# Last units of the hidden layer put in another order, the reload of db cut into eight, and the transform's middle multiplied through a negated plane

## The chip, the cores and the metric

The kernel runs on one core of one Trainium2 chip. The metric is the time of one execution on the device in microseconds (us); the runs of the kernel before took 1208.77, 1212.85 and 1214.51 us, median 1212.85.

The engines go by the profile's names: PE multiplies matrices (PEld is its weight load), DVE works on vectors, ACT copies and evaluates functions, POOL does vector work and issues the stores, and SP issues the loads. Each engine takes its instructions strictly in order. A transposing load issued by SP appears in SP's row with a long duration, and what SP issues next stands behind it.

## What is computed

The forward value and all gradients of a gated sum of a spectral filter and a two-layer perceptron, 2048 rows by 1024 columns, hidden width 3584, bfloat16 in and out:

```python
g = sigmoid((x * gate_w).sum(-1, keepdims=True))
a = irfft2(rfft2(x.astype(float32)) * (w_r + 1j * w_i))
h = relu(x @ w1 + b1); h = h * h
b = h @ w2 + b2            # here x is B_x, with no gradient
out = g * a + (1 - g) * b
_, vjp = jax.vjp(f, A_x, w_r, w_i, w1, b1, w2, b2, gate_w); vjp(grad_out)
```

## The kernel before, in words

**The stages.** The rows of x and of the incoming gradient come in, are turned for the matmuls, and the row transforms of the spectral part write z_scr in DRAM; db, the gradient that goes into the perceptron, is stored to db_scr. Then the *hidden layer* runs (`mlp_in`, one generator) and beside it, step by step, the spectral part (`fft_mid`, then `fft_out`). After it the gradients of w1 and w2 and the output of the second layer are made (`mlp_grads`), from h2T_scr and dhT_scr, the hidden values and their gradients, which the hidden layer has stored. The "first pass" is the hidden layer, the "second pass" what comes after it.

**The hidden layer.** The hidden width is 28 chunks of 128, that is 14 pairs `fp` (0 to 13, `LAST` is 13). Rows are 4 blocks `s` of 512, that is 2 halves `sp`. Pairs 0 and 1, and half 0 of the last pair, are made plainly (`forth`, L740). The others go in *units* `(fp, sp)` of seven chains (`p1` to `p7`, L847), a Strassen-like scheme: each unit multiplies sums of quarters of w1 (`w_sums`, L836, four sums on DVE per pair) with sums of quarters of x (`x_sums`), and DVE's `rest` (L863) adds the pieces and the bias into `rT`. With it come, for the unit before, four `pd` chains of eight matmuls (`grads`, L747), which DVE evicts into `dhT` (L751). The order written out is `seq`: (2,0), (2,1), (3,0) ... (12,0), (12,1), (13,1). The sums for an odd pair lie in the last two rows of the tile `dbn`, those of x in the rest: while the units run, dbn (16 row blocks of db) is lent out as `kept`, and after them it is loaded again from db_scr (`again`, L1001): rows 0 to 7 after unit (12,0), rows 8 to 15 after the last unit. Each w1 pair is loaded into w1g (L769) one pair ahead, two buffers.

**What runs beside it.** The middle of the transform, `fft_mid`, makes 32 turns `(m, h)`, 16 pairs of frequencies by two halves. A turn loads z (L393, SP), makes sum and difference `pm` (L413, L414, DVE), multiplies on PE to `px` (L422), copies to x on ACT (L423, and an edge column, L424), multiplies x with the filter w on DVE into tt (L430 with the real part, L431 with imaginary and negated imaginary), joins the products to y (L441, L442; the column at the edge by L438, L439), goes back through PE (L450) to pc (ACT L455, DVE L456, L457), and makes the gradients of the filter (L467 to L471, two products and two sums), which ACT scales into gw. The planes of x are real and imaginary, each of 2 x 256 values and two edge columns.

**What sets the order.** `spread` lets one generator make steps while the other runs, at a given rate of steps per step of the hidden layer, so a step of the transform falls between two chains of a unit. Within an engine the order of the program, as adjusted by explicit ties such as `later["last"]`, is the order of execution. SP takes loads in that order: z, w1g, the transposing loads of w2 (`load_w2`, L183), the reload of db, and the first transposing loads of the second pass (`fetch` from h2T_scr, four into `even` and four into `odd`, also L183). The loads into `even` wait for `later["blocks"]`, the last dhT eviction made within unit (12,0), which the loop of the units sets.

The second pass begins with PE chains on dbn and `even` (L1143, pX and pV), and sums T and S of dbn and `even` on DVE (L1075).

Of the kernel before, what the change touches and what calls it, by code (L numbers as in the profile page):

```python
# [10 lines left out]
P = 128  # L11
BF16 = mybir.dt.bfloat16
FP16 = mybir.dt.float16
FP32 = mybir.dt.float32
ALU = mybir.AluOpType
ACT = mybir.ActivationFunctionType

FDT = FP16
# [123 lines left out]
def kernel(  # L142
# [22 lines left out]
    nc = tc.nc  # L165
# [9 lines left out]
    NT = S // P  # L175
# [8 lines left out]
    ld, st = nc.sync.dma_start, nc.gpsimd.dma_start  # L184
    V, mm = nc.vector.tensor_tensor, nc.tensor.matmul
# [18 lines left out]

    identb = pers.tile([P, P], BF16, name="identb", tag="identb")
    nc.scalar.dma_start(out=identb[:], in_=cten["identb"].ap())
    kf = pers.tile([P, 2, P], FDT, name="kf", tag="kf")
    flip = pers.tile([P, 1], FP32, name="flip", tag="flip")
    cols = lambda n, w, dt=FP32: pers.tile([P] + w, dt, name=n, tag=n)
    gcol, omg, gpg, dgs, dsc = (cols(n, [NT]) for n in ("gcol", "omg", "gpg", "dgs", "dsc"))  # L210
# [114 lines left out]
    def fft_mid(filler):  # L325
# [6 lines left out]

        def edges():

            ed = fb.tile([P, NM, 2, 4], FDT, name="ed", tag="ed")
            low = fb.tile([P, NM, 4], FDT, name="low", tag="low")
            mid = fb.tile([P, 4], FDT, name="mid", tag="mid")
            nc.vector.memset(ed[lanes[1], 0], 0.0)
            col = z_scr[:].rearrange("t c r x h l -> r c h l x t")[:, :, 0, 0]
            for x in range(2):  # L340
                for t in range(2):
                    e = 2 * x + t
                    st(out=ed[lanes[0], :, 0, e], in_=col[:, 0:NM, x, t])
                    st(out=low[lanes[1], :, e], in_=col[:, NM:, 1 - x, t])
                    st(out=mid[lanes[0], e : e + 1], in_=col[:, NM, 1 - x, t : t + 1])
            return ed, low, mid
# [10 lines left out]
        def edges_through(ams, ed, low, mid):  # L357
            tied = lambda ins: after(ins, later["last"], mybir.DependencyClass.NoSync)
            tied(nc.vector.tensor_copy(out=ed[lanes[0], :, 1, :], in_=ed[lanes[0], :, 0, :]))
            tied(nc.vector.tensor_copy(out=ed[lanes[0], 0, 1, :], in_=mid[lanes[0]]))  # L360
            for n in range(2):
                a, b = slice(2 * n, 2 * n + 2), slice(2 - 2 * n, 4 - 2 * n)
                tied(nc.vector.tensor_copy(out=ed[lanes[1], 1:, n, a], in_=low[lanes[1], 1:, a]))
                tied(nc.vector.tensor_scalar(out=ed[lanes[1], 1:, n, b], in0=low[lanes[1], 1:, b], scalar1=-1.0, scalar2=None, op0=ALU.mult))
            sp = fps.tile([P, NM, 2, 4], FP32, name="sp", tag="ps2", bufs=2)
            for h in range(2):
                for m in range(NM // 2):
                    for n in range(2):
                        mm(
                            sp[:, h * NM // 2 + m, n], lhsT=ams[h][:, m, n, :], rhs=ed[:, h * NM // 2 + m, n, :],  # L370
                            start=True, stop=True, skip_group_check=True,
                        )
            ex = fb.tile([P, NM, 2, 2, 2], FDT, name="ex", tag="ex")
            for n in range(2):
                for c in range(2):
                    nc.vector.tensor_copy(
                        out=ex[lanes[n], :, c], in_=sp[lanes[c], :, n, :].rearrange("p m (e t) -> p m t e", e=2)
                    )
            return ex

        def filters(m):
# [33 lines left out]
            return pm  # L415

        def transform(m, h, pm, ex):
            x = fb.tile([P, 2, 2, WL], FDT, name="x", tag="x", bufs=2)
            px = fps.tile([P, 2, 2, HW], FP32, name="px", tag="ps2", bufs=2)
            for c in range(2):  # L420
                for n in range(2):
                    behind(mm(px[lanes[n], c], lhsT=mats[m][:, 0, n, lanes[c]], rhs=pm[:, n], start=True, stop=True), "PE")  # L422
            nc.scalar.copy(out=x[:, :, :, 0:HW], in_=px[:])  # L423
            nc.scalar.copy(out=x[:, :, :, h * HW], in_=ex[:, m, :, :, h])  # L424
            return x

        def products(h, x, w):
            tt = fb.tile([P, 2, 2, 2, WL], FDT, name="tt", tag="tt")
            W = HW + h
            V(out=tt[:, 0, :, :, 0:W], in0=x[:, :, :, 0:W], in1=w[:, 0:1, 0:W].rearrange("p (o t) l -> p o t l", o=1).to_broadcast([P, 2, 2, W]), op=ALU.mult)  # L430
            V(out=tt[:, 1, :, :, 0:W], in0=x[:, :, :, 0:W], in1=w[:, 1:3, 0:W].rearrange("p (o t) l -> p o t l", o=1).to_broadcast([P, 2, 2, W]), op=ALU.mult)  # L431
            return tt

        def joined(h, tt, eh):
            if h:
                nc.scalar.copy(out=eh[:], in_=tt[:, :, :, :, HW])
            else:
                V(out=tt[:, :, 0, :, 0], in0=tt[:, :, 0, :, 0], in1=eh[:, :, 1, :], op=ALU.subtract)  # L438
                V(out=tt[:, :, 1, :, 0], in0=tt[:, :, 1, :, 0], in1=eh[:, :, 0, :], op=ALU.add)  # L439
            y = fb.tile([P, 2, 2, HW], FDT, name="y", tag="y")  # L440
            V(out=y[:, 0], in0=tt[:, 0, 0, :, 0:HW], in1=tt[:, 1, 1, :, 0:HW], op=ALU.subtract)  # L441
            V(out=y[:, 1], in0=tt[:, 0, 1, :, 0:HW], in1=tt[:, 1, 0, :, 0:HW], op=ALU.add)  # L442
            return y

        def back(m, h, y):
# [15 lines left out]

        def grads_of_w(h, x):
            W = HW + h
            XA, XB = (x[:, :, T, 0:W] for T in range(2))
            gs = fb.tile([P, 2, WL], FDT, name="gs", tag="gs", bufs=2)
            t1_ = fb.tile([P, 2, WL], FDT, name="g1", tag="g1")
            V(out=t1_[:, :, 0:W], in0=XB, in1=XA, op=ALU.mult)  # L467
            V(out=gs[:, 0, 0:W], in0=t1_[:, 0, 0:W], in1=t1_[:, 1, 0:W], op=ALU.add)
            t2_ = fb.tile([P, 2, WL], FDT, name="g1", tag="g1")
            V(out=t2_[:, :, 0:W], in0=XB, in1=XA[:, ::-1, :], op=ALU.mult)  # L470
            V(out=gs[:, 1, 0:W], in0=t2_[:, 1, 0:W], in1=t2_[:, 0, 0:W], op=ALU.subtract)  # L471
            return gs

        def grads_out(m, h, gs, gw, done):
# [25 lines left out]
        yield  # L500
        for u, (m, h) in enumerate(turns):
            if h:
                eh = fb.tile([P, 2, 2, 2], FDT, name="eh", tag="eh")
            x = transform(m, h, pm, ex)
            yield
            if u + 1 < len(turns):
                pm = mirrored(turns[u + 1][0], z.pop(u + 1))
            if held:
                done = back(*turns[u - 1], held)
            tt = products(h, x, w)  # L510
            if u + 1 < len(turns):
                m2, h2 = turns[u + 1]
                w = by_groups(h2, wn[m2])
            yield
            held = joined(h, tt, eh)
            yield
            if u:
                grads_out(*turns[u - 1], gs, gw, done)
            gs = grads_of_w(h, x)
            if h:  # L520
                gw = fb.tile([P, 2, LW], BF16, name="gw", tag="gw", bufs=2)
                if m + 1 < NM:
                    wn[m + 1] = filters(m + 1)
            if u + 2 < len(turns):
                z[u + 2] = inputs(*turns[u + 2])
            yield
# [113 lines left out]
    f1, f1_s = pool("f1", "right")  # L640

    cf = f1.tile(list(consts["cf"].shape), FDT, name="cf", tag="cf")
    xs = {}

    def turn_tile(dst, i, src, copy):
# [61 lines left out]
    def mlp_in():  # L707
# [227 lines left out]
                load_w1(2)  # L935
        for _ in w_sums(2, True):
            pass
        seq = [(fp, sp) for fp in range(2, LAST) for sp in range(2)] + [(LAST, 1)]
        more_sums = x_sums(1)
        units_ = [Unit(*u) for u in seq]  # L940
        units_[0].p2()
        for n, u in enumerate(units_):
            fg, pr = divmod(u.fp, NPR)
            if u.sp == 0 and u.fp < LAST:
                load_w1(u.fp + 1)
            u.p1()
            if n:
                units_[n - 1].square(0, u.copy)
            back_(*waiting[0])
            u.p5()  # L950
            yield
            next(more_sums, None)
            u.p6()
            if n:
                units_[n - 1].square(1, u.copy)
            back_(*waiting[1])
            next(more_sums, None)
            ahead_ = w_sums(u.fp + 1, True) if u.sp == 1 and u.fp < LAST else iter(())
            next(ahead_, None)
            yield  # L960
            u.p7()
            back_(*waiting[2])
            next(more_sums, None)
            next(ahead_, None)
            yield
            back_(*waiting[3])
            for _ in ahead_:
# [8 lines left out]
            elif n == 2 * DC + 1:  # L976
                grad_of_b2()
            u.p4()
            u.p3()
            if n + 1 < len(units_):  # L980
                units_[n + 1].p2()
            yield
            waiting = [(u.fp, 2 * u.sp + j, c) for c, j in ((0, 0), (0, 1), (1, 1), (1, 0))]
            if (u.fp, u.sp) == (LAST - 1, 0):
                again(slice(0, 8))
        again(slice(8, NT))
        units_[-1].square(0), units_[-1].square(1)
        more = [(LAST, s, c) for c in range(2) for s in range(2)]
        for this, that in zip(more, waiting):
# [7 lines left out]
        wbs.close()  # L997
        xT_s.close()

    def again(rows_):  # L1000
        ld(out=dbn[:, rows_, :], in_=db_scr[:, rows_, :])  # L1001

    def column_sums(sb_pool, acc, tag):

# [837 lines left out]
```

## Time and profile before

| what | value |
|---|---|
| median of three runs | 1212.85 us (1208.77 to 1214.51) |
| the profiled execution, its own time | 1206.2 us |
| its span, first to last instruction | 1204.4 us |
| mean granted TensorE clock | 0.999 |
| busy PEld, share of the span | 637.2 us, 53% |
| DMA moved | 249.88 MB, mean 207 GB/s |
| loads: z 128 KB, w1g 512 KB, db 2048 KB | 4.1, 5.1, 9.9 us median from issue to landing |

A row of a timeline or queue gives the start in us from the span's beginning, the duration, the engine, the line, the operation, the tile written and those read, and in brackets the idle time just before and what ended it. A row of waits gives who waited for whom, the us in total, how often and the longest. A group of instructions gives after the count the busy time in us, the mean of one in ns and the idle time ahead.

### The profile page before, as it was taken

Reading aid. Unit: us, or ns where it says so; the run is one execution under the profiler, and the core shown is the slowest. Engines: PE = TensorE matmul, PEld = TensorE weight load, DVE = VectorE, ACT = ScalarE, POOL = GpSimd, SP = SyncE. Lnnn points to the kernel's source line nnn. Section 1 sums busy time; section 2 is a strip of 40 time slices with the busy share of each in tenths; the row PEclk is TensorE's granted clock in tenths of the full one; section 3 lists DMA queues with packets and bytes.
Section 4 is the critical chain, followed back from the end, with each engine's and each line's share of the span. In section 5 each row is a group of like instructions: output and inputs, shape, how many; then the busy total and the mean of one; then the engine's idle time right before and its main releaser. Section 6 shows DMA issues by size and latency. Waiting matters only on the chain.

```text
span 1204.4 us, 19697 instructions
## 1 busy us (share of the span) xinstructions
PE 1184.8 (98%) x7379; PEld 637.2 (53%) x7379; DVE 886.4 (74%) x1660; ACT 513.2 (43%) x909; POOL 381.9 (32%) x614
## 2 busy tenths in 40 slices
PE   8999999999999998999999999999999999999997
PEld 5565555444344433444446999998544444444444
DVE  3668887589999878777736666666785777977666
ACT  4668888466666663334423566564110110000000
POOL 0223333766666654564341323321001100000000
PEclk9999999999999999999999999999999999999999
DMA  9977575967585899899995999995899999564531
GB/s 287 302 247 227 168 218 159 202 194 202 175 206 177 248 228 246 177 178 230 197 239 126 238 225 250 238 214 161 255 206 273 270 230 273 161 195 144 184 114 36
DMA packets 328986, 249.88 MB, mean 207 GB/s; under 512 B 188200, under 2 KB 287946, under 8 KB 328122
## 3 DMA queue, kind: packets, MB, share of 16 engines
q1 hardware_dynamic: 283808, 119.99, 46.3%
q0 software_dynamic: 35520, 111.74, 29.4%
q10 hardware_dynamic: 9562, 16.89, 4.3%
q8 instruction: 58, 0.95, 0.3%
q14 instruction: 38, 0.31, 0.1%
HBM read 114.84 MB, written 89.67 MB: 170 GB/s over the span
## 4 chain that ended last, share of the span: by engine, by line
PE 74%; DVE 12%; DMA 5%; issue 3%; ACT 3%; SPq 1%; POOL 1%; DVEq 0%; POOLq 0%
PE pX L1143 15%; PE xX L1439 13%; PE pV L1143 11%; PE pd L747 10%; PE xV L1439 7%; PE ph L847 6%; PE xZ L1439 3%; DMA y_scr<-pc 2%; PE ph L740 1%; PE pui L317 1%; PE pki L576 1%; PE pZ L847 1%; PE pu L317 1%; PE px L422 1%; PE pk L286 1%
## 5 line engine op out<-in xcount | busy, mean ns | idle before, releaser
L747 PE MATMUL pd<-dbT,w2T 128*128 128x512 bf16 x896 | 211.0, 379 | 5.0 <-DVE dhT L751 3.9
L747 PEld LDWEIGHTS <-w2T 128*128 128x128 bf16 x896 | 85.7, 98 | 109.9 <-issue 12.3
L1439 PEld LDWEIGHTS <-dS 128*128 128x128 f16 x686 | 66.5, 98 | 78.6 <-issue 3.0
L751 DVE SCALAR_TENSOR_TENSOR dhT<-pd,rT 128x512 bf16<-128x512 f32 x112 | 76.6, 685 | 41.4 <-PE pd L747 39.3
L1490 POOL DMA_DIRECT2D out_dram<-ot x32 | 17.3, 542 | 257.1 <-DVE ot L1546 128.0
L1556 ACT ACTIVATE w2br<-w2br,dsc 128x512 f32<-128x512 bf16 x8 | 5.8, 723 | 172.8 <-DVE ot L1546 117.4
L1439 PE MATMUL xX<-oT,dS 128*128 128x512 f16 x336 | 76.4, 379 | 0.2 <-DVE eR L1468 0.2
L1159 ACT COPY u<-pX 128x512 f32<-128x512 f32 x56 | 32.8, 585 | 93.2 <-PE pX L1143 87.1
L1439 PEld LDWEIGHTS <-odd 128*128 128x128 bf16 (+1 forms) x462 | 44.8, 98 | 51.5 <-issue 0.9
L1439 PEld LDWEIGHTS <-even 128*128 128x128 bf16 (+1 forms) x448 | 43.7, 98 | 52.6 <-issue 0.7
L1143 PEld LDWEIGHTS <-T 128*128 128x128 f16 x672 | 64.4, 98 | 8.2 <-DVE S L1075 1.2
L864 ACT ACTIVATE rT<-rT 128x512 bf16<-128x512 bf16 x69 | 43.3, 628 | 51.2 <-DVE rT L863 51.0
L732 ACT ACTIVATE h2T<-rT 128x1024 bf16<-128x1024 bf16 x56 | 59.7, 1066 | 0.5 <-DMA h2T_scr<-h2T 0.2
L459 POOL DMA_DIRECT2D y_scr<-pc x64 | 47.0, 736 | 36.7 <-DVE pc L456 28.3
L1163 DVE TENSOR_TENSOR whi<-pV,u 128x512 bf16<-128x512 f32 x28 | 19.3, 690 | 51.0 <-ACT u L1159 50.9
L1143 PEld LDWEIGHTS <-S 128*128 128x128 f16 x336 | 31.8, 98 | 43.2 <-DVE S L1075 3.3
L1143 PEld LDWEIGHTS <-resL 128*128 128x128 bf16 x448 | 43.1, 98 | 4.9
L1143 PEld LDWEIGHTS <-resR 128*128 128x128 f16 (+1 forms) x448 | 42.9, 98 | 5.1 <-issue 0.2
L778 POOL DMA_DIRECT2D h2T_scr<-h2T x28 | 20.6, 736 | 73.6 <-ACT f L274 35.7
L232 POOL DMA_DIRECT2D r<-y_scr x48 | 27.9, 584 | 42.8 <-ACT re L555 27.4
L1143 PEld LDWEIGHTS <-even 128*128 128x128 bf16 (+1 forms) x256 | 24.6, 98 | 31.0 <-issue 2.1
L484 POOL DMA_DIRECT2D out_dram<-gw x64 | 34.3, 541 | 17.3 <-ACT gw L480 10.9
(375 smaller groups left out, 2765.3 us busy)
## 6 DMA issues: line engine op xcount, KB each, us to landing
h2T_scr<-h2T POOLq DMA_DIRECT2D x28, 512.0 KB, 4.4
dhT_scr<-dhT POOLq DMA_DIRECT2D x28, 512.0 KB, 5.6
z<-z_scr SPq DMA_DIRECT2D x64, 128.0 KB, 4.1
y_scr<-pc POOLq DMA_DIRECT2D x64, 128.0 KB, 4.2
ax_scr<-yo POOLq DMA_DIRECT2D x16, 512.0 KB, 5.4
out_dram<-ot POOLq DMA_DIRECT2D x31, 256.0 KB, 3.8
out_dram<-whi POOLq DMA_DIRECT2D x28, 256.0 KB, 5.4
out_dram<-wlo POOLq DMA_DIRECT2D x28, 256.0 KB, 4.6
```

Of the source, the lines that this page charges most:

```text
L232: st(out=a, in_=b) if stored else st(out=b, in_=a)
L317: first_ = mm(pu[:, bank, lo : lo + n], lhsT=ft[:, b, :], rhs=mat[:, o : o + n], start=bool(f_ & 1), stop=bool(f_ & 2), skip_group_check=True,
L459: st(out=columns_of(y_scr, c, h), in_=pc[:, n])
L484: st(out=every(dst_w, k), in_=gw[lanes[n], c_, 0:W1])
L732: after(nc.scalar.activation(h2T, rT, ACT.Square), behind_, mybir.DependencyClass.NoSync)
L747: mm(pd[:], lhsT=w_[:, ec, fc % FGC * P : (fc % FGC + 1) * P], rhs=dbT[:, ec, ss], start=(ec == 0), stop=(ec == DC - 1),)
L751: return STT(out=dhT, in0=pd[:], scalar=2.0, in1=rT, op0=ALU.mult, op1=ALU.mult, accum_out=gb1part[:, fc, sb : sb + 1],)
L847: mm(acc[:], lhsT=lhs[:, t, :], rhs=rhs[:, t, :], start=start and t == 0, stop=t == KH - 1, skip_group_check=True)
L864: nc.scalar.activation(rT, rT, ACT.Relu)
L1143: self.mm = mm(out, lhsT=lhs[:, t, m * P : (m + 1) * P], rhs=rhs[:, t, :], start=start and t + a == 0, stop=t == KH - 1, skip_group_check= ...
L1159: turn["ACT"] = nc.scalar.copy(out=t_[:], in_=self.X[:])
L1439: ins = mm(acc, lhsT=lhs[:, fc, :], rhs=rhs[:, fc, :], start=start and fc == 0, stop=fc == KH - 1 and bias is None, skip_group_check=True,)
```

## The change

Three things are changed; what is computed stays the same. `kf`, a small constant, also moves from a lasting pool to one that ends with the first stage, and the scratch tiles of `edges` now use space of others.

**Units.** The last units run as (10,0), (10,1), (11,0), (12,0), (11,1), (12,1), (13,1). The load of w1g for pair 13 is therefore issued at unit (11,1).

**Reload.** dbn comes back in eight pieces of two row blocks, as the sums in them have been read: four after the chains of unit (12,0)'s successor (11,1), three during the last unit, and one behind it.

**Transform.** x has three planes: negated imaginary, real, imaginary. The negated one is one more ACT multiply of px. The products take planes (real, imaginary) with the real part of the filter, and (negated imaginary, real) with its imaginary part, so that y is one sum of 1024 values. The edge column is joined first (`en`) and added to y once. The gradients of the filter take one product of 1024 values and one sum.

```diff
-        seq = [(fp, sp) for fp in range(2, LAST) for sp in range(2)] + [(LAST, 1)]
+        seq = [(fp, sp) for fp in range(2, LAST - 2) for sp in range(2)]
+        seq += [(fp, sp) for sp in range(2) for fp in (LAST - 2, LAST - 1)] + [(LAST, 1)]
+        freed = seq.index((LAST - 1, 0))
+        def freed_rows(n, low, high):
+            if n == freed + 1:
+                again(slice(2 * low, 2 * low + 2), later["last"])
+            elif n == len(seq) - 1 and high:
+                again(slice(6 + 2 * high, 8 + 2 * high))
...
-            if u.sp == 0 and u.fp < LAST:
+            if (u.fp, u.sp) == (LAST - 2, 1):
+                load_w1(LAST)
+            elif u.sp == 0 and u.fp < LAST - 1:
                 load_w1(u.fp + 1)
...
             u.p5()
+            freed_rows(n, 0, 1)
             yield
             next(more_sums, None)
             u.p6()
+            freed_rows(n, 1, 2)
...
-            ahead_ = w_sums(u.fp + 1, True) if u.sp == 1 and u.fp < LAST else iter(())
-            next(ahead_, None)
+            follows = u.fp + 1 if u.sp == 1 and u.fp < LAST - 2 else {(LAST - 2, 0): LAST - 1, (LAST - 1, 1): LAST}.get((u.fp, u.sp))
+            ahead_ = w_sums(follows, True) if follows else iter(())
+            dealt = ahead_ if (u.fp, u.sp) != (LAST - 2, 0) else iter(())
+            next(dealt, None)
...
+            freed_rows(n, 2, 0)
...
             u.p4()
+            freed_rows(n, 3, 3)
...
-            if (u.fp, u.sp) == (LAST - 1, 0):
-                again(slice(0, 8))
-        again(slice(8, NT))
+        again(slice(NT - 2, NT))
```
```diff
         def transform(m, h, pm, ex):
-            x = fb.tile([P, 2, 2, WL], FDT, name="x", tag="x", bufs=2)
+            x = fb.tile([P, 3, 2, WL], FDT, name="x", tag="x", bufs=2)
...
-            nc.scalar.copy(out=x[:, :, :, 0:HW], in_=px[:])
+            nc.scalar.copy(out=x[:, 1:3, :, 0:HW], in_=px[:])
+            nc.scalar.mul(out=x[:, 0, :, 0:HW], in_=px[:, 1], mul=-1.0)
...
         def joined(h, tt, eh):
+            V(out=y[:], in0=tt[:, 0, :, :, 0:HW], in1=tt[:, 1, :, :, 0:HW], op=ALU.add)
             if h:
-                nc.scalar.copy(out=eh[:], in_=tt[:, :, :, :, HW])
+                V(out=en[:], in0=tt[:, 0, :, :, HW], in1=tt[:, 1, :, :, HW], op=ALU.add)
+                nc.scalar.mul(out=eh[:, 0], in_=en[:, 1], mul=-1.0)
+                nc.scalar.copy(out=eh[:, 1], in_=en[:, 0])
             else:
-                V(out=tt[:, :, 0, :, 0], in0=tt[:, :, 0, :, 0], in1=eh[:, :, 1, :], op=ALU.subtract)
-                V(out=tt[:, :, 1, :, 0], in0=tt[:, :, 1, :, 0], in1=eh[:, :, 0, :], op=ALU.add)
-            V(out=y[:, 0], in0=tt[:, 0, 0, :, 0:HW], in1=tt[:, 1, 1, :, 0:HW], op=ALU.subtract)
-            V(out=y[:, 1], in0=tt[:, 0, 1, :, 0:HW], in1=tt[:, 1, 0, :, 0:HW], op=ALU.add)
+                V(out=y[:, :, :, 0], in0=y[:, :, :, 0], in1=eh[:], op=ALU.add)
...
         def grads_of_w(h, x):
-            V(out=t1_[:, :, 0:W], in0=XB, in1=XA, op=ALU.mult)
-            V(out=gs[:, 0, 0:W], in0=t1_[:, 0, 0:W], in1=t1_[:, 1, 0:W], op=ALU.add)
-            V(out=t2_[:, :, 0:W], in0=XB, in1=XA[:, ::-1, :], op=ALU.mult)
-            V(out=gs[:, 1, 0:W], in0=t2_[:, 1, 0:W], in1=t2_[:, 0, 0:W], op=ALU.subtract)
+            V(out=t_[:, :, :, 0:W], in0=XB, in1=XA, op=ALU.mult)
+            V(out=gs[:, ::-1, 0:W], in0=t_[:, :, 0, 0:W], in1=t_[:, :, 1, 0:W], op=ALU.add)
```

## Prediction

> **What bounds the kernel now.** I read the share of busy time first, then who makes TensorE (PE) wait, then 20 us windows around the change, then the queues there. PE is busy 1184.8 of 1204.4 us at a granted clock of 0.999, and no step of the diff alters a matmul's count or shape. So a gain can only come out of PE's 19.6 us of idle time. From the idle time noted in PE's timeline, 3.4 lie in the first 12 us and 7.0 after 1196 us, untouched by the change. About 9.2 are left, in small pieces but for one place: the window from 440 to 460 us holds 3.92 (20 minus 16.08). The page, the waits of PE and the windows:
>
> ```profile
> PE 1184.8 (98%) x7379; PEld 637.2 (53%) x7379; DVE 886.4 (74%) x1660; ACT 513.2 (43%) x909; POOL 381.9 (32%) x614
> ```
> ```profile
> PE pd L747 <- DVE dhT L751: 3.9, 2, 3.3
> PE pX L1143 <- DVE S L1075: 1.6, 3, 0.7
> PE pd L747 <- DVE rT L863: 1.1, 3, 0.6
> ```
> ```profile
> 420.00:440.00 20.00, 20.00 (x100) 7.91 (x97) 17.16 (x44) 14.79 (x25) 11.62 (x18) 1.00 1.23 170
> 440.00:460.00 20.00, 16.08 (x76) 6.88 (x75) 12.30 (x32) 7.78 (x14) 11.26 (x19) 1.00 1.10 316
> ```
>
> The windows' columns are stretch, length, then busy time of PE, PEld, DVE, ACT and POOL: PE is full until 440, and DVE too drops to 12.30 after it. The reason stands in the queue of the loads (SP), start and duration first:
>
> ```profile
> 404.95 0.33 SPq L1001 DMA_DIRECT2D dbn<-db_scr  x1
> 405.63 8.94 SPq L183 DMA_TRANSPOSE even<-h2T_scr  x1
> 414.68 1.96 SPq L393 DMA_DIRECT2D z<-z_scr  x2
> 416.68 21.53 SPq L183 DMA_TRANSPOSE even<-h2T_scr  x3
> 438.31 2.60 SPq L393 DMA_DIRECT2D z<-z_scr  x4
> ```
>
> Four transposing loads hold SP for 8.94 + 21.53 = 30.4 us. The z loads behind them issue only at 438.31; DVE stands for them, with the hidden layer's evictions (dhT, L751) queued behind, and PE stands for those. DVE's and PE's timelines:
>
> ```profile
> 445.20 0.43 DVE L413 TENSOR_TENSOR pm<-z 128x512 f16<-128x512 f16 x1 [5.36 <-DMA z<-z_scr]
> ...
> 456.39 0.68 DVE L751 SCALAR_TENSOR_TENSOR dhT<-pd,rT 128x512 bf16<-128x512 f32 x1
> ```
> ```profile
> 450.24 3.61 PE L747 MATMUL pd<-dbT,w2T 128*128 128x512 bf16 x16 [0.65 <-DVE dhT L751]
> 457.13 5.34 PE L747 MATMUL pd<-dbT,w2T 128*128 128x512 bf16 x24 [3.27 <-DVE dhT L751]
> ```
>
> **Part 1, order of units and reload in pieces.** The four transposes wait for the dhT of unit (12,0), which comes one unit (about 15 us) earlier. In SP's new order they start near 389 us, back to back; behind them come pieces 1 and 2, two z loads, piece 3, the load of w1g for pair 13, and then pieces and z in turn. The z loads of 438.31 now stand behind no transpose: they issue by about 430 and are needed at 439 to 447. So the 5.36 us wait of DVE goes, and with it the stall: **-3.9 us** on PE. What is late next there: between two dhT stand only two pm and two tt, about 2.2 us of DVE, against 1.7 us of a pd chain with other matmuls between; I leave nothing.
>
> The cost sits in w1g for 13. In before it issues at 390.42, ahead of the transposes. Now it stands behind all four, and its sums (L836) are in DVE's order as before, the first at 415.24. When do four transposes end that start at 389? Pairs of them elsewhere in SP's timeline:
>
> ```profile
> 285.24 6.86 SPq L183 DMA_TRANSPOSE w2T<-in_B_w_dram  x2
> 345.26 7.97 SPq L183 DMA_TRANSPOSE w2T<-in_B_w_dram  x2
> ```
>
> Two such pairs give 14.8 us, ending near 404; the four odd transposes at 453.11 took 20.07, giving 409; the 30.4 us of 405 to 438 gives 419.4. I take 16 to 20 us, as the 280 to 350 pairs stand in the same stage of units. With pieces and z before it, w1g issues at 406 to 411, and lands at its median of 5.1 us, or 7 behind pieces: 411 to 418. PE does not feel it until about 417.9: what stands behind the sums is rT (L863, 416.42), needed for the chain at 419.65, and the dhT at 417.75, needed near 420.5. I take **+0.6 us** (bounds 0 and, from 30.4 us, w1g issued at 421.5 and landed at 428 to 431, +10 to +13).
>
> The eight pieces: issue costs 0.33 to 0.70 us each on SP, which waits anyway. The two 2 MB loads took 9.9 us to land. The first reader of dbn as db is PE's pX at 462.94, and the last piece issues when the last sums are read, about 435.5. Even the 9.9 us of four times the size after that is 445: 17 us of cover, so nothing. If a piece were delayed past 462, it would cost one for one.
>
> The rows of the DMA issues give a load of w1g (512 KB) a median of 5.1 us to landing and one of db (2048 KB) 9.9: four times the data in twice the time, so small pieces do cost more per byte. The Trainium skill, "DMA: Bandwidth & Descriptors", section "Bandwidth", advises batching transfers to 1 MiB or more, which speaks against eight of 512 KB and agrees with those rows. By the fit in that page's section "Anatomy of one DMA" (an estimate) eight would take about 26 us of transfer against 14 for two of 2 MB; if that were on the path the sum would be 12 us worse.
>
> **Part 2, transform with a negated plane.** Per turn (32 turns) DVE loses one y, two g/gs and, on average, no edge operation. The rows of the groups (mean ns after the busy time):
>
> ```profile
> L441 DVE TENSOR_TENSOR y<-tt 128x512 f16<-128x512 f16 x32 | 14.2, 443 | 0.0
> L442 DVE TENSOR_TENSOR y<-tt 128x512 f16<-128x512 f16 x32 | 13.7, 429 | 0.0
> L598 DVE TENSOR_TENSOR tt<-ev,e 128x1024 f16<-128x1024 f16 x16 | 11.1, 691 | 1.5
> ```
>
> 443 + 429 become one like L598, 691 ns: 0.18 saved. Two products g (418 and 431 at h=0) and two sums gs (286 and 340) become one of about 690 and one of about 440: 1475 to 1130, 0.35 saved. At h=0 one of two edge fixes (417, 166) goes; at h=1 one is added. Records overlap by about 0.08, so some 0.25 us a turn, 8 us of DVE in all. DVE is 74% busy and PE does not wait for it but at the places named: **0** on the path. Only the stall near 396 us (0.59, pd waits for rT, the third row of the waits) stands behind a run of such operations, and rT comes 1 to 2 us earlier: **-0.6**.
>
> ACT gains one 128x512 multiply out of PSUM and small copies: L455's 582 ns plus about 0.2, 26 us in all. ACT was 13 to 15 of 20 us busy in the stage, and its own work is not waited for by PE. But the two products now need the negated plane, so x is ready about 0.6 us later; DVE idled at L430 for ACT 4.1 us in 32 turns, and other DVE work stands between. Bounds: 0, and 32 x 0.6 = 19 us if every turn exposed it to PE; the nearest row is the 1.1 us that PE ever waited for rT, so I take 0.
>
> Two places where DVE's new order is worse. (a) At 246.95 pm waits 0.82 for z, issued behind transposes:
>
> ```profile
> 243.90 0.74 DVE L863 SCALAR_TENSOR_TENSOR rT<-pZ,b1col,cu 128x512 bf16<-128x512 f32 x1
> ...
> 246.95 0.81 DVE L413 TENSOR_TENSOR pm<-z 128x512 f16<-128x512 f16 x1 [0.82 <-DMA z<-z_scr]
> ```
>
> In the built order of the changed kernel that pm comes before rT (pZ) and dhT, since the products are fewer. If z lands as before, rT ends at 248.1 where PE's pd took its bank at 245.69: **+2.4 us** (bounds 0, if z is early, and 2.4). (b) At the start of the second pass y, pc, pc, the edge fix, g and gs (about 1.0 us more than before) now come ahead of T and S, whose end PE awaits at 473.61 (0.67 idle): **+1.0 us** (bounds 0 and 1.7).
>
> **Sum.** 1206.2 (the profiled execution; span 1204.4) - 3.9 - 0.6 + 0.6 + 2.4 + 1.0 = 1205.7, or -0.5. The median of the three runs is 1212.85, 6.65 above the profiled one; the difference is laid on the median: **1212.3 us**. About 0.5%, 6 us, is what a measurement here can tell from no change.
>
> **Rivals.** *Nothing new is late (faster).* z is early at 246, T and S come as before, w1g is early: -4.5; if small waits of the middle (9.2 in all, less the 4.5) halve too, -6.9, so 1206. For it: DVE is freed of 8 us. Against: those pieces lie in many places with other releasers, and 6 us is two thirds of all there is.
> *The transposes hold SP as they do now (slower).* w1g for 13 issues at 421.5, lands at 428 to 431, DVE stands at L836 with rT and dhT behind it, and PE for those: +10 to +13 in place of +0.6, so 1222 to 1225. It is slower by over 0.5% once w1g lands after about 424. For it: the four are the same loads of h2T_scr that took 30.4, now with stores and 2 MB of w2T traffic near. Against: in before they ran beside a 2 MB reload from 404.95, and pairs elsewhere took 7 to 8.
> *The change doesn't do what it says.* A piece holds SP and z is still late at 440: the 3.9 stay, so 1216.2.
>
> **Chances.** Forecast 0.50; transposes slow 0.24; nothing late 0.14; z still late 0.12. The first and last lie within 0.5% (1206.8 to 1218.9): same 0.62, faster 0.14, slower 0.24. The range runs from 1206, the faster rival's end, to 1223, within the slower rival's, which leaves out about 0.2.
>
> **What would show it.** Right: no long idle at L413 near 445, pd at 457 without a wait, four transposes within 20 us from 389, w1g landed before 418, a new PE wait of about 2 us near 246 for rT. Wrong: L836 waiting for w1g by more than 3 us, or PE waiting for x (L423) or pm in many turns, which would put ACT's added 0.6 us on the path.

## The result, and the profile after

The changed kernel takes 1222.95 us (median; 1220.89 to 1225.95) against 1212.31 for the one before, a ratio of 1.0109 with a 95% interval of 1.0086 to 1.0133: **slower by 1.1%**. Its profiled execution has a span of 1220.6 us at a clock of 0.991, 16.2 us more than before's 1204.4 at 0.999. The rival "the transposes hold SP as they do now" came true, not the forecast. Some executions here fall into a slower state with a lower granted clock: the ratios leave them out, the medians given beside the ratios do not, and of the two profiles that fell into it (`split_first` and `transform_w2split`) only rows before 430 us are used.

The medians differ by 10.6 us, less than the spans: before's profiled execution took 1206.2, which is 6.1 under its median, the changed kernel's 1222.39, 0.6 under.

The page's first line, the waits of PE, and the windows (columns as before), all of the changed kernel:

```profile
PE 1187.0 (97%) x7379; PEld 637.8 (52%) x7379; DVE 873.6 (72%) x1564; ACT 530.4 (43%) x958; POOL 381.3 (31%) x614
```
```profile
PE ph L854 <- DVE rT L870: 14.9, 1, 14.9
PE pd L754 <- DVE rT L870: 2.7, 2, 2.3
PE pX L1165 <- DVE S L1097: 2.1, 3, 1.4
```
```profile
420.00:440.00 20.00, 5.09 (x18) 1.52 (x16) 5.69 (x16) 1.69 (x3) 3.84 (x7) 0.62 0.86 229
440.00:460.00 20.00, 20.00 (x96) 7.83 (x93) 16.12 (x35) 15.54 (x27) 14.04 (x22) 0.96 0.87 252
```

The hole of 3.92 us between 440 and 460 is gone, and so is the wait of pd for dhT (L758 now). In its place PE stands empty for one wait of 14.9 us between 420 and 440, and the granted clock falls with it (0.62, then 0.96). PE's busy time rises by 2.2 us though it does the same matmuls. The queue of loads (SP) shows what is ahead of what:

```profile
391.37 28.26 SPq L183 DMA_TRANSPOSE even<-h2T_scr  x4
419.72 1.26 SPq L1023 DMA_DIRECT2D dbn<-db_scr  x2
421.07 1.10 SPq L397 DMA_DIRECT2D z<-z_scr  x2
422.26 0.47 SPq L1023 DMA_DIRECT2D dbn<-db_scr  x1
422.83 0.40 SPq L776 DMA_DIRECT2D w1g<-in_B_w_dram  x1
```

The same load stood in before at 390.42, ahead of the transposes. It lands 11.5 us after its issue. DVE and PE, in turn:

```profile
434.31 0.42 DVE L843 TENSOR_TENSOR dbn<-w1g 128x512 f16<-128x512 bf16 x1 [17.08 <-DMA w1g<-in_B_w_dram]
434.66 0.69 DVE L442 TENSOR_TENSOR y<-tt 128x1024 f16<-128x1024 f16 x1
435.26 0.75 DVE L870 SCALAR_TENSOR_TENSOR rT<-ph,b1col,cu 128x512 bf16<-128x512 f32 x1
```
```profile
436.06 1.86 PE L854 MATMUL ph<-xT,Sw 128*128 128x512 bf16 x4 [14.91 <-DVE rT L870]
```

DVE stands 17.08 us at the first sum of w1g (the prediction's L836). Behind it in DVE's order is the rT that frees PE's bank, and PE waits for that. The chain has three links, and only the first, the load, is late by itself. The four matmuls after the wait take 1.86 us where four took 1.03 in before.

The difference of the spans adds up from rows: +14.9 (this wait), +2.3 (near 246 us), +1.0 (first sums of the second pass), +2.2 (PE's longer busy time), -3.9 and -0.6 (the two waits that went): +15.9 of 16.2.

One correction to the text on the kernel: SP does not simply follow the order in which the program names the loads. `fetch` is called after all units, yet its transposes stand among the units' loads; their place is set by what they are tied to, `later["blocks"]`.

### The profile page after: what moved, and what is told of

It reads as the page before. It is cut to its first block, busy times and chain, and to the rows that moved or that the text cites. A ratio compares the mean times of both kernels' runs of the same rounds, so it can differ in the third digit from the quotient of the medians.

```text
span 1220.6 us, 19674 instructions
## 1 busy us (share of the span) xinstructions
PE 1187.0 (97%) x7379; PEld 637.8 (52%) x7379; DVE 873.6 (72%) x1564; ACT 530.4 (43%) x958; POOL 381.3 (31%) x614
## 4 chain that ended last, share of the span: by engine, by line
PE 77%; DVE 9%; DMA 4%; SPq 4%; issue 2%; ACT 2%; POOL 0%; DVEq 0%; POOLq 0%
PE pX L1165 14%; PE xX L1461 13%; PE pd L754 12%; PE pV L1165 10%; PE ph L854 7%; PE xV L1461 6%; SPq L183 3%; PE xZ L1461 3%; PE ph L747 2%; PE pui L316 1%; PE pZ L854 1%; PE pki L582 1%; PE pv L457 1%; PE pu L316 1%; PE px L426 1%
## 5 line engine op out<-in xcount | busy, mean ns | idle before, releaser
L758 DVE SCALAR_TENSOR_TENSOR dhT<-pd,rT 128x512 bf16<-128x512 f32 x112 | 76.8, 685 | 47.0 <-PE pd L754 45.0
L437 DVE TENSOR_TENSOR tt<-x,w 128x1028 f16<-128x1028 f16 (+1 forms) x64 | 42.1, 690 | 8.3 <-issue 6.1
```

The lines of the kernel that those rows point to most:

```text
L437: V(out=tt[:, k, :, :, 0:W], in0=x[:, a : a + 2, :, 0:W], in1=by, op=ALU.mult)
L758: return STT(out=dhT, in0=pd[:], scalar=2.0, in1=rT, op0=ALU.mult, op1=ALU.mult, accum_out=gb1part[:, fc, sb : sb + 1],)
```

## The experiments

**Which half of the change costs?** Two kernels: `transform_only` has the hunks of the transform (with `kf` and `edges`), `units_only` those of the units and the reload.

> Only the edit of the transform (three planes, merged products and sums); units and reload as in the kernel before. Theory A (the loss is the late load of w1g for the last pair, behind four transposes): the stall of about 15 us is not there; PE's idle near 246 us grows by 2.3 and that ahead of the second pass's sums by 0.8, the z wait near 445 stays or shrinks: 1212 to 1216. Theory B (the edit of the transform is what slows it, because ACT hands out x later and DVE is in another order): 1218 to 1224, spread over many turns.

> Only the order of the units and the reload in eight pieces; the transform as in the kernel before. Theory A: a PE stall of 13 to 16 us for rT behind the sums of w1g, w1g landing near 434, and none of the 2.3 at 246: 1218 to 1222. Theory B: the stall is small once DVE's order is the old one: under 1214.

`transform_only`: 1205.65 us, ratio 0.9955 (0.9938 to 0.9972), faster. `units_only`: 1216.26, ratio 1.0044 (1.0031 to 1.0058), slower. So theory B falls: the edit of the transform helps, beyond what theory A expected of it. PE's waits with the transform alone:

```profile
PE pd L754 <- DVE rT L870: 3.5, 3, 2.7
PE pX L1150 <- DVE S L1082: 1.9, 2, 1.4
```

The 2.7 near 246 us and the 1.4 at the sums came, as forecast; PE's waits list none at the `px` and `pv` chains, where a later x would show, and the wait for dhT near 457 us is absent. In that execution z stood behind the transposes as in before, but they held SP for 9.44 + 15.50 = 24.9 us instead of 30.5 (27.2 against 32.0 when both kernels were profiled once more), so that z issued at 434.63 instead of 438.31; whether the edit made them shorter is open. With the units alone the stall is there without any edit of the transform:

```profile
389.34 25.12 SPq L183 DMA_TRANSPOSE even<-h2T_scr  x4
...
417.60 0.38 SPq L769 DMA_DIRECT2D w1g<-in_B_w_dram  x1
```
```profile
429.90 1.87 PE L847 MATMUL ph<-xT,Sw 128*128 128x512 bf16 x4 [11.37 <-DVE rT L863]
```

It is smaller than theory A had it (13 to 16, w1g near 434): 11.4, with w1g at 428.6, and so the time lies under A's 1218 to 1222.

**Is it the transposes ahead of w1g, or the pieces?** Two single edits of the changed kernel.

```diff
-        after(ld(out=dbn[:, rows_, :], in_=db_scr[:, rows_, :]), earlier)
+        piece = ld(out=dbn[:, rows_, :], in_=db_scr[:, rows_, :])   # w1g_first
+        after(piece, earlier)
+        after(piece, later["w1"], mybir.DependencyClass.NoSync)
```
```diff
-            after(turned(...), later["blocks"])
+            after(turned(...), later["blocks2" if (n, i) == (0, 1) else "blocks"])   # split
```

(`later["w1"]` is the last load of w1g; `blocks2` is set in unit (12,1).)

> The changed kernel with one edit: the load of w1g for the last pair is issued ahead of the db pieces (still behind the four transposes). Theory A with two terms (the hold of the four transposes, and the landing slowed by 1.5 MB of pieces ahead): issued at 421, landed in 5 to 7 us instead of 11.5, the stall falls from 14.9 to 8 to 10: 1216 to 1219. If the pieces do not matter for the landing: 11 us again, 1222 to 1224.

> The changed kernel with one edit: two of the four transposes wait for a later unit, so that w1g for the last pair stands behind two. Theory A (four back to back hold the queue as one short and three full ones; two as one short and one full): the pair holds SP for 8 to 14 us from 391, w1g issues when its buffer is free near 406 and lands by 417: the stall of 15 us and the slower clock after it are gone: 1205 to 1209. If it is the pieces or the wait for the buffer that make w1g late: a stall of 5 us or more stays, 1212 or more.

Both missed: PE's wait is 17.6 us in `w1g_first` and 7.7 in `split`. `w1g_first`: 1226.34 us, ratio 1.0121 (1.0095 to 1.0146). The load did go ahead of the pieces, but the four transposes held SP for 33.46 us this time, so it issued at 429.47; it landed 10.3 us later, at 439.8. `split`: 1215.99 us, ratio 1.0045 (1.0031 to 1.0058); two transposes held SP for 14.01, w1g issued at 410.28 as expected, and landed only at 428.8:

```profile
428.82 0.43 DVE L843 TENSOR_TENSOR dbn<-w1g 128x512 f16<-128x512 bf16 x1 [9.91 <-DMA w1g<-in_B_w_dram]
```

An early issue was not an early landing. The packets in the trace say why: on the queue of SP's loads, the transposes' packets (256 bytes) run first, then the pieces' (4096 bytes), then w1g's (512 bytes). They begin in the order of issue and overlap at the seams (in `split`, w1g's run partly beside those of the piece issued behind it). In the changed kernel the transposes' last packet starts at 423.0 and w1g lands 11.3 us after it, with 1.5 MB of pieces between; in `w1g_first` the last one starts at 433.7 and w1g lands 6.1 after it. So the pieces were worth about 5 us of landing, the transposes the rest. `w1g_first` was not faster for it, because its transposes' packets took 37.8 us (395.9 to 433.7) against 30.1 in the changed kernel (392.9 to 423.0); why, no run shows. SP's row shows when a transpose was issued; the data come after.

**Both edits together, and the size of the pieces.** `split_first` has both; `split_first_two` reloads db in two loads of 2 MB (rows 0 to 7 in unit (11,1), rows 8 to 15 at the end) in place of eight of 512 KB.

> The changed kernel with both edits: two of the four transposes later, and w1g for the last pair issued ahead of the db pieces. Theory C (loads of one queue are served in order, so w1g lands when all that was issued ahead of it on SP is through: the transposes' data, then 1.5 MB of pieces): w1g lands near 416 to 419 instead of 428.8, the stall of 7.7 falls to 0 to 2 and the clock stays at 1: 1206 to 1209. If the DMA engines as a whole are the limit, whoever stands ahead: a stall of 5 or more stays, 1213 or more.

> As the one before, but db comes back in two loads of 2 MB (one after the first chains that follow the release of rows 0 to 7, one at the end of the units) instead of eight of 512 KB. If the size of the pieces costs transfer time that someone waits for: faster than split_first by 1 to 4 us. If the reload is hidden either way: the same within 2 us, unless the second load, which now starts at the end, holds up the sums of the second pass: then slower by 1 to 4.

`split_first`: 1213.6 us, ratio 1.0008 (0.9984 to 1.0032); `split_first_two`: 1212.3, ratio 1.0018 (0.9996 to 1.0040). The stall shrinks, 7.7 to 4.4 and 4.1, but neither to the 0 to 2 of theory C nor does it stay at the 5 or more of its rival. Even two transposes ahead put w1g's landing at 425.7 and 424.6:

```profile
393.21 15.21 SPq L183 DMA_TRANSPOSE even<-h2T_scr  x2
408.53 1.70 SPq L397 DMA_DIRECT2D z<-z_scr  x2
410.27 0.86 SPq L776 DMA_DIRECT2D w1g<-in_B_w_dram  x1
```

The order on SP's queue is not the whole of it. In `split_first_two` no piece stood ahead of w1g, and still 9.2 us passed from the transposes' last packet (415.4) to its landing (424.6); from 417 to 420 us POOL's queue moved over 200 KB per us beside it. In the changed kernel POOL's stores land late too while the transposes run. Its stores issued from 330 to 390 us, and those from 392 to 421 (size of one, median us from issue to landing):

```profile
h2T_scr<-h2T POOLq DMA_DIRECT2D x4, 512.0 KB, 4.0
y_scr<-pc POOLq DMA_DIRECT2D x12, 128.0 KB, 2.7
```
```profile
h2T_scr<-h2T POOLq DMA_DIRECT2D x2, 512.0 KB, 10.6
y_scr<-pc POOLq DMA_DIRECT2D x6, 128.0 KB, 11.4
```

The late landings move with the transposes: in before they are those issued from 405 to 437 us (9.7 and 8.4), in `w1g_ahead` those from 416 to 447 (11.3 and 12.2). So the other queue is slowed as well, and w1g issued from another engine would probably not have been free of them; no run tries it.

Two loads or eight cannot be told apart: each ratio is known to 0.0024 either way, some 3 us. The rule of the Trainium skill that the prediction cited ("DMA: Bandwidth & Descriptors", section "Bandwidth", batch to 1 MiB or more) is neither shown nor contradicted by this. The fit from which the prediction took its 12 us (section "Anatomy of one DMA") is given there for DMAs issued by GpSimd; these are issued by SP.

**w1g ahead of all transposes.** `w1g_ahead` ties all four, and the pieces as in `w1g_first`, behind w1g; `w1g_then_turned` ties only the transposes, so that three pieces stay ahead of it.

```diff
-            after(turned(...), later["blocks"])
+            last_ = turned(...)
+            after(last_, later["blocks"])
+            if n == 0:
+                after(last_, later["w1"], mybir.DependencyClass.NoSync)
```

> The changed kernel with one edit: on SP the load of w1g for the last pair stands ahead of the pieces and of all four transposes. Theory C (one queue, served in order; the transposes' 2 MB take about 30 us): w1g issues near 406 and lands by 415, so no stall for the sums and no lower clock: 16 us of after's span go, and what z then waits behind the transposes near 440 costs 0 to 4: 1205 to 1210. If the loss is in the order of the units or in the pieces themselves: 1215 or more.

> The same, but three db pieces (1.5 MB) stay ahead of w1g; only the transposes are behind it. If the pieces ahead cost w1g some 4 us of landing, as the packets of the runs so far say: it lands at 412 to 418, PE loses 0 to 1: 1206 to 1210, hardly apart from w1g_ahead. If the pieces were the larger part of the 15 us: a stall of 5 or more, 1213 or more.

`w1g_ahead`: 1211.46 us, ratio 1.0011 (0.9990 to 1.0032). `w1g_then_turned`: 1208.95, ratio 0.9991 (0.9971 to 1.0010), w1g landed in 6.3 us:

```profile
407.44 0.37 SPq L776 DMA_DIRECT2D w1g<-in_B_w_dram  x1
407.91 0.66 SPq L1023 DMA_DIRECT2D dbn<-db_scr  x1
408.61 14.58 SPq L183 DMA_TRANSPOSE even<-h2T_scr  x2
```
```profile
418.22 0.48 DVE L843 TENSOR_TENSOR dbn<-w1g 128x512 f16<-128x512 bf16 x1
```

In both the wait for w1g is gone, with the order of the units and the eight pieces in place: **it was the place of this load behind the transposes**. But not all of the gain stays, and `w1g_ahead` missed its 1205 to 1210. In it the transposes now stand ahead of z, and SP and DVE read as in before, only worse:

```profile
416.37 32.04 SPq L183 DMA_TRANSPOSE even<-h2T_scr  x4
448.51 1.10 SPq L397 DMA_DIRECT2D z<-z_scr  x2
```
```profile
453.88 0.42 DVE L417 TENSOR_TENSOR pm<-z 128x512 f16<-128x512 f16 x1 [10.10 <-DMA z<-z_scr]
```

PE loses 3.2 us to pm and 2.6 to dhT there. In `w1g_then_turned` two z loads stand between the transposes, and DVE still waits 5.96 and 8.16 us for z. Whichever load stands behind the four transposes can pay for their 30 us: z in before, w1g in the changed kernel, z again here. It need not: with the transform alone z stood behind them, and PE did not wait.

**The stall near 246 us.** A w2T load also has two transposes; `w2split` loads one half in each of the two units of a pair (`load_w2` now takes the halves to load). Added to the transform alone, and to `w1g_ahead`:

```diff
-                if 0 < fg < FG - 1:
-                    load_w2(fg + 1, later["last"])
+            if pr == 0 and 0 < fg < FG - 1:
+                load_w2(fg + 1, later["last"], (u.sp,))
```

> Only the edit of the transform, and each w2T load of two transposes cut into one per unit, so that z stands behind one. If the stall near 246 us is z behind two transposes: the 2.7 us there go, 1202 to 1204. If z is late there for another reason (its stores, the DMA engines): no change from the transform alone, 1205 to 1206.

> w1g_ahead with the two transposes of each w2T load in different units, so that z near 246 us stands behind one: 2 to 3 us of PE's idle time there go, 1202 to 1207. If z stays late there: as w1g_ahead.

`transform_w2split`: 1204.96 us, ratio 0.9941 (0.9920 to 0.9963), the lowest median here; `w1g_ahead_w2split`: 1209.95, ratio 0.9991 (0.9978 to 1.0005), not the 1202 to 1207 expected. In both the 2.5 to 2.7 us of PE waiting for rT near 246 are gone, so it was z behind two transposes. The medians are 0.7 and 1.5 us below those without the edit, which the intervals do not tell from nothing.

**Both references once more.**

> The kernel before, profiled once more. If its profiled execution was a typical one: z waits near 445 and PE stalls of 3 to 5 us there, span 1204 to 1208. If that stall varies from run to run with the time that four transposes hold SP, and so makes the median of before: a stall there of 5 to 10 us and a span near 1208 to 1210.

> The edit of the transform alone, once more, beside the three others: again 1204 to 1207. If the order of the units and the reload in pieces are worth something once w1g is in time, w1g_ahead is faster than this one; if they only cost, slower.

`before_again` has a span of 1205.6 us at a clock of 0.999 and 5.3 us of waits for dhT near 457; a second execution like the first. `transform_only_2`: 1206.48 us, ratio 0.9968 (0.9954 to 0.9982). `w1g_ahead`, run beside it, is 5 us slower (1.0011, 0.9990 to 1.0032), and the intervals do not overlap. So with w1g in time the order of the units and the eight pieces still cost: the transform alone is already without the stall that they were to remove, and in `w1g_ahead` DVE waits 10.10 us for z.

## Why the prediction was wrong

**The step that failed is the +0.6 us for w1g.** It has two parts. First, "Two such pairs give 14.8 us ... I take 16 to 20 us": four transposes held SP for 28.26. A pair's hold does not scale so. Inside one the first issue is short:

```profile
285.24 2.66 SPq L183 DMA_TRANSPOSE w2T<-in_B_w_dram  x1
```

That is the first of the pair of 6.86 in before, and it could have been read there: 2.66 for the first, 4.16 for the second. In the changed kernel the four take 3.75, 9.85, 8.20 and 6.34. Only the first is issued with nothing large ahead of it. Each later one holds SP for 6 to 10 us, and its issue ends (405.0, 413.3, 419.6) one to three us after the packets of the one ahead have ended (403.2, 410.2, 418.5). In before, with a 2 MB load just ahead, the first took 8.94 as well. Two pairs contain two short ones, four in a row only one. And the very same four loads had shown 30.4 us in before; they were the nearest row, and I set them aside because a 2 MB reload ran beside them. Without that reload they took 25 to 33.

Second, the landing: 11.5 us, not 5.1 to 7. A median of landings is that of a queue with little ahead; here the tail of the transposes and 1.5 MB of pieces stood ahead. The slower rival, priced at +10 to +13 with a landing at 428 to 431, had the chain right, place by place; the landing came at 434.3 and the wait was 14.9. That its 1222 to 1225 holds the measured 1222.95 is in part luck: by the rows the change costs 15.9 us, more than it had priced, but the medians differ by only 10.6. It lacked **the clock**, which no term of the sum held: 2 to 3 us more.

```profile
424.70:436.00 11.30, 0.00 (x0) 0.00 (x0) 1.69 (x5) 0.00 (x0) 0.00 (x0) 0.50 1.02 307
436.00:441.70 5.70, 5.64 (x15) 1.55 (x15) 5.70 (x16) 2.79 (x6) 1.31 (x2) 0.50 0.23 67
```

In these windows of the changed kernel the clock is at 0.50 for the rest of the wait, and stays so for 5.7 us in which PE works again: at half speed, some 2.8 us lost.

**The other steps held.** The stall of 3.9 at 457 us went, and so did the 0.59 at 396. The new wait near 246, forecast at 2.4, is 2.34; the DVE row shows it as forecast, pm ahead of the rT that PE waits for:

```profile
247.42 0.42 DVE L417 TENSOR_TENSOR pm<-z 128x512 f16<-128x512 f16 x1 [3.41 <-DMA z<-z_scr]
247.77 0.74 DVE L870 SCALAR_TENSOR_TENSOR rT<-pZ,b1col,cu 128x512 bf16<-128x512 f32 x1
```

The sums of the second pass: 0.67 became 1.44 plus 0.22 for `even`, +1.0 as forecast. DVE lost 12.8 us of busy time (forecast 8), ACT gained 17 (forecast 26), and neither reached PE. The pieces' transfers were hidden from their own readers, as costed, but not from what stood behind them on SP: about 5 us of w1g's landing. That is the cost that "so nothing" left out.

**The two halves do not add.** The product of their ratios is 1.0044 x 0.9955 = 0.9999, against 1.0109 for both. Two reasons are in the rows: each half alone removes the 3.9 us stall, which can be saved only once, and the wait for w1g is 14.9 with both and 11.4 with the units alone. That is 7.4 us. In the spans the halves give -0.6 and +9.7 and both together +16.2, which leaves 7.1, so these two account for it. The ratios leave some 13 us; the rest stands only in the medians, and I have not tied it to rows.

**Open.** The transform alone is 4 to 5 us faster in the medians, but only 0.6 in the spans of the profiles (1203.8 against 1204.4). Of the 82 executions of the kernel before that enter the ratios of the experiments, the 8 at a mean clock of 0.999 have a median of 1207.7 us, the 16 at 0.995 or less 1213.5; both profiled ones are at 0.999. One stretch of 3.41 us at half clock takes 0.0014 off the mean clock and costs PE up to 1.7 us, so from 0.999 to 0.995 it is about three stretches, up to 5 us of the 5.8 (an estimate from these numbers). So its profile probably shows an execution in which its stall near 457 us drew no half clock, and the others often have that on top. This is argued from the clocks of the runs, not shown in a trace.

## What to carry to other kernels

When a change moves a load on a queue, price it by everything that stands ahead of it on that queue until the data are through, and by what other queues move at the time, not by the issue's own row and not by a median landing. For N long transfers back to back, take the row of the same N, or one short and N-1 full ones (all full, if something large is already ahead); several short groups elsewhere do not add up to a long one. And when a queue is held for 30 us, reordering mainly chooses who waits: ask which load behind it has the least slack. Spreading the long transfers removed the wait near 246 us here, but only part of the one near 430. Two edits that remove the same stall pay once.

## What the runs showed of the hardware

**A short gap can cost a stretch of half clock, and the same gap may not.** The trace's clock records hold the half clock for 17.07 us in the changed kernel, 13.65 in `units_only`, 6.83 in `split`, 3.41 near 251 us in `w1g_first`: 5, 4, 2 and 1 times 3.41. The last followed a PE wait of only 2.29 us:

```profile
247.60:251.10 3.50, 1.23 (x6) 0.58 (x6) 2.37 (x7) 0.63 (x1) 2.31 (x4) 1.00 0.77 233
251.10:254.50 3.40, 3.40 (x12) 0.77 (x10) 1.99 (x6) 2.98 (x7) 0.80 (x1) 0.50 0.29 83
```

The changed kernel's wait of 2.34 at the same place drew none, nor did before's of 3.27. The Trainium skill, "TensorE: Matmul & The Clock Gate", section "Part 1: The HAM clock gate", states a free-running window of 3413 ns and half rate after an idle one. The lengths agree. But the window ahead of the drop here, 247.60 to 251.10, was busy for 1.23 of 3.50 us, so less than a wholly idle one sufficed.

The traces show how much did. Count windows of 3.413 us (17.07 / 5) from each trace's first rise to full clock, and add up PE's idle time in each. In the twelve profiles other than `split_first` and `transform_w2split`, every one of the 11 drops before the last 25 us of the span came right after a window with about 2.0 us or more of idle time (1.997 at the least), and no window without a drop had more than 2.08. So in these traces it matters where a gap falls. The 2.29 us of `w1g_first` lie almost wholly in one window (2.22 idle); the 2.34 of the changed kernel fall across an edge (0.94 and 1.40), and so do before's 3.27 (1.34 and 1.93).

**A transposing load is slow, and its queue is held.** The four bring 2 MB in 8192 packets of 256 bytes and take 30.1 us from the first packet to the last in the changed kernel (26.0 in `units_only`, 37.8 in `w1g_first`); a plain load of 2 MB from db_scr landed in 9.9 us in before. While they run, stores of another queue take some two to four times as long to land (10.6 and 11.4 us in place of 4.0 and 2.7).
